# An attention and two-layer mixture-of-experts kernel: VectorE finishes a pair's first block before it converts weights, and the second layer's routing steps move between quarters

## The chip, the core and the metric

The kernel runs on one core of a Trainium2 chip. The metric is device time in microseconds (us) of one execution. Engines are named as in the profile: PE (TensorE), DVE (VectorE), ACT (ScalarE), POOL (GpSimd) and SP (SyncE, which issues the DMAs).

## What is computed

Decayed causal attention over 4608 tokens makes x (4608 x 512). Two mixture-of-experts layers follow. In each a token goes to one of eight experts (the largest of eight logits). Cut to what matters:

```python
def _moe_ref(x, w_gate, w_output_gate, w1, w2):
    logits = x @ w_gate
    e_idx = np.argmax(logits, axis=1)
    ...
    for e in range(E):                       # E = 8, D = 512, F = 1024
        mask = e_idx == e
        h = np.maximum(x[mask] @ w1[e], 0.0)
        ye = h @ w2[e]
        out[mask] = gate_w[mask, None] * eom[mask, e, None] * ye

def reference(**kwargs):
    ...
    x = _moe_ref(x=x, **moe_kwargs)
    return _moe2_ref(x=x, **moe2_kwargs)     # as above, with a bias by modality
```

So the second layer's experts are chosen from the first layer's output, token by token.

## The kernel before

Attention and the first layer's routing take the first 225 us; the change does not touch them. Then `experts` runs sixteen positions `P_`, eight experts of the first layer (`P_ < E`) and eight of the second, with an instruction stream written out per engine; engines meet only in counting semaphores (`take` waits for one and takes it down).

A position's rows are worked in **units**: a pair of 128-row blocks in slot 0, a pair in slot 1, and, where a block is left over, a short unit (slot 2). In these inputs every expert of the first layer has two pairs and a short unit, but expert 5, which has no short unit. A unit goes like this:

- PE computes `ph = w1.x` in four quarters (`quarter(g)`, each 24 matmuls of 256 columns; L991 to L993), then `py = h.w2` for block 0 (`second(0, ...)`, in four parts q of 6 matmuls, part q waiting for quarter q's `h_full`) and for block 1 (`second(1, ...)`; L999 to L1001).
- For each quarter ACT writes the ReLU (L1093) and signals `hh_full`; DVE then evicts the rest into `hT` (L1205) and signals `h_full`. Both engines go through the quarters in order, with other work between.
- `back` ends a block in the first layer: ACT squares `py` (L1081, `ss_full`), DVE makes a scale (`eb`, `v_s`, `f_full`), ACT writes the upper half of the output row (L1084, `x2h_full`), DVE the lower half and signals `x2_rdy`. ACT does not go on to the next block or unit before DVE's `f_full`. In the second layer DVE's part is `final`, three small instructions.
- SP waits for `x2_rdy` and transposes the row back on chip as `x2T`, for the second layer's routing.

**The second layer's routing** of a unit's blocks runs inside the next unit, in four steps: PE's `logits` (L969, needs `x2T`), DVE's `choose` (six small instructions; it gives `l2_full` to ACT and `oh_full` to PE), ACT's `gate` (an exponential), PE's `ranks` (L974, L975, needs `oh_full`) and DVE's `place` (needs `rk_full` from the ranks). `routed` says at which point of a unit each step stands: points 0 to 3 follow quarter g, points 4 to 7 follow part q of `second(0)`. Before the change ACT's and DVE's steps stand at the quarter of the logits.

**Weights** of the next position come in four quarters c of 1 MB into `stg`. ACT makes the upper half (`conv`, L1070), DVE the lower (`conv`, `wb<-stg,wb` of 128 x 2048), which frees that part of `stg` for SP's next load. In slot 0 ACT and DVE convert c = 0 and 1, in slot 1 c = 2 and 3 (`brought`). SP works in program order too: a load that waits for `stg` holds up the transposes behind it.

In slot 0 DVE does both conversions after the fourth eviction and before `back` of block 0:

```python
for q in range(2 - (slot or 0)):
    brought(ve, R_, P_, conv, slot, q + (slot or 0))
if routing or asked(P_, slot):
    ve.sem_inc(T["cnt_ask"])
for b in range(blocks[s]):
    back(s, b) if P_ < E else final(s, b)
```

Of the kernel before, what the change touches and what calls it, by code (L numbers as in the profile page):

```python
# [490 lines left out]
def experts(nc, st, I, K, out):  # L491
# [225 lines left out]
            for q in range(2):  # L717
                brought(eng, R_, P_, conv, 1, q)

    def routed(eng, was, s, sure, at, fn, what=0):  # L720


        plan = {"short": ((1, 3), (3, 7)), "first": ((1, 2), (2, 4), (3, 7)), "pair": (None, (1, 2), (3, 7))}
        for k, p in enumerate(plan["short" if s == 2 else "pair" if sure else "first"]):
            if p and (at is None or p[what] == at):
                if k == 1 or sure:
                    fn(k // 2)
                else:
                    with when(eng, was, "EQ", 2 - k // 2):
                        fn(1)  # L730

    def behind(P_, slot):

# [28 lines left out]
    with nc.Block() as block:  # L762
# [197 lines left out]
        def _(pe):  # L960
            with ExitStack() as rs:
# [20 lines left out]
                def unit(P_, s, w, sure, slot=None, routing=None, counting=False):  # L982
                    two, cs = s < 2, cols(P_, w)
                    if routing is None:
                        routing = behind(P_, slot)

                    def quarter(g):
                        for f in (2 * g, 2 * g + 1):
                            fs, o = slice(f * P, f * P + P), ph[g][:, f % 2, cs]
                            for c in range(4):  # L990
                                pe.matmul(o, w1(P_, 0)[:, c, fs], xT[s][:, c, cs], start=(c == 0), stop=False)  # L991
                                pe.matmul(o, w1(P_, 0)[:, c, fs], xT[s][:, 4 + c, cs], start=False, stop=False)  # L992
                                m = pe.matmul(o, w1(P_, 1)[:, c, fs], xT[s][:, c, cs], start=False, stop=(c == 3))  # L993
                        m.then_inc(T["ph_full"])

                    def second(b, fs):
                        bs = slice(b * P, b * P + P)
                        for f in fs:
                            pe.matmul(py[b], hT[:, 0, f, bs], w2(P_, 0)[:, f, :], start=(f == 0), stop=False)  # L999
                            pe.matmul(py[b], hT[:, 0, f, bs], w2(P_, 1)[:, f, :], start=False, stop=False)  # L1000
                            m = pe.matmul(py[b], hT[:, 1, f, bs], w2(P_, 0)[:, f, :], start=False, stop=(f == 7))  # L1001
                        if f == 7:
                            m.then_inc(T["py_full"])

                    def route(at):
                        if routing:
                            routed(pe, was, s, sure, at, ranks, 1)
                            routed(pe, was, s, sure, at, logits)
                    take(pe, f"x_full{s}", 16)
                    for g in range(4):  # L1010
                        quarter(g)
                        route(g)
                    take(pe, "py_free0")
                    for q in range(4):
                        take(pe, "h_full")
                        if P_ == 0 and q in (0, 2):
                            pe.wait_ge(T[f"w0_full{2 + q // 2}"], 1)
                        second(0, (2 * q, 2 * q + 1))
                        route(4 + q)
                    if P_ < E:  # L1020
                        note(pe, was, s, sure)
                    if two:
                        take(pe, "py_free1")
                        second(1, range(4))
                        if counting:
                            counts(cum)
                        if slot == 0:
                            ahead(pe, R_, P_)
                        second(1, range(4, 8))
                        if asked(P_, slot):  # L1030
                            counts(cums)
# [5 lines left out]
                for P_ in range(NP):  # L1037
                    if P_ == E - 1:
                        take(pe, "ord_pe")
                        learn(pe, R_)  # L1040
                    if P_ == E:
                        take(pe, "w_full", 4)
                        with when(pe, R_["early"], "GT", 0):
                            for k in range(EP):
                                unit(E, k, PAIR, False, routing=k == 0, counting=k == 0)
                        with pe.Else():
                            routed(pe, was, 0, False, None, lambda b: (logits(b), ranks(b)))
                            counts(cum)
                        take(pe, "reg_pe")
                        less_early(pe, R_)  # L1050
                    co.leave(R_, P_)
                    if P_ and P_ != E:
                        take(pe, "w_full", 4)

                    def none(P_=P_):
                        ahead(pe, R_, P_)
                        if P_ == E - 2:
                            counts(cums)
                    walk(co, R_, P_, unit, none)
# [3 lines left out]
        def _(ac):  # L1063
            with ExitStack() as rs:
# [24 lines left out]
                def unit(P_, s, w, sure, slot=None, routing=None):  # L1089
                    cs = cols(P_, w)  # L1090
                    for g in range(4):
                        take(ac, "ph_full")
                        ac.activation(hT[:, 0, 2 * g:2 * g + 2, cs], ph[g][:, :, cs], AF.Relu).then_inc(T["hh_full"])  # L1093
                        if P_ == 0 and slot == 0 and g < 2:
                            conv(0, 2 + g)
                        brought(ac, R_, P_, conv, slot, {(0, 2): 0, (1, 0): 0, (1, 2): 1}.get((slot, g)))
                        if routing or behind(P_, slot):
                            routed(ac, was, s, sure, g, gate)
                    if slot == 0:
                        brought(ac, R_, P_, conv, slot, 1)  # L1100
                    ac.sem_inc(T[f"x_free{s}"])
                    for b in range(blocks[s]):
                        back(P_, s, b)
                    if P_ < E:
                        note(ac, was, s, sure)
# [6 lines left out]
                for P_ in range(NP):  # L1112
                    if P_ == E - 1:
                        take(ac, "ord_ac")
                        learn(ac, R_)
                    if P_ == E:
                        with when(ac, R_["early"], "GT", 0):
                            for k in range(EP):
                                unit(E, k, PAIR, False, routing=k == 0)
                        with ac.Else():  # L1120
                            routed(ac, was, 0, False, None, gate)
                        take(ac, "reg_ac")
                        less_early(ac, R_)
                    co.leave(R_, P_)
                    ahead(ac, R_, P_)
                    walk(co, R_, P_, unit, conv=conv)
# [3 lines left out]
        def _(ve):  # L1130
            ch = Chain(ve, T, "dve")
            tt, ts, stt, tr = ve.tensor_tensor, ve.tensor_scalar, ve.scalar_tensor_tensor, ve.tensor_reduce
            with ExitStack() as rs:
# [64 lines left out]
                def unit(P_, s, w, sure, slot=None, routing=None):  # L1198
                    cs = cols(P_, w)
                    for g in range(4):  # L1200
                        routes = routing or behind(P_, slot)
                        if routes and g < 3:
                            routed(ve, was, s, sure, g, choose)
                        take(ve, "hh_full")
                        stt(hT[:, 1, 2 * g:2 * g + 2, cs], ph[g][:, :, cs], 0.0, hT[:, 0, 2 * g:2 * g + 2, cs], op0=ALU.max, op1=ALU.subtract).then_inc(T["h_full"])  # L1205
                        if routes:
                            if g == 3:
                                routed(ve, was, s, sure, g, choose)
                            routed(ve, was, s, sure, g, place)
                        if P_ == 0 and slot == 0 and g < 2:  # L1210
                            conv(0, 2 + g)
                        if slot == 1 and g == 1:
                            brought(ve, R_, P_, conv, slot, 0)
                    for q in range(2 - (slot or 0)):
                        brought(ve, R_, P_, conv, slot, q + (slot or 0))
                    if routing or asked(P_, slot):
                        ve.sem_inc(T["cnt_ask"])
                    for b in range(blocks[s]):
                        back(s, b) if P_ < E else final(s, b)
                    if asked(P_, slot):  # L1220
                        order()
                    if P_ < E:
# [57 lines left out]
                for P_ in range(NP):  # L1280
# [5 lines left out]
                    if P_ == E:  # L1286
# [2 lines left out]
                            final_counts()  # L1289
                            unit(E, 1, PAIR, False)  # L1290
                        with ve.Else():
                            routed(ve, was, 0, False, None, lambda b: (choose(b), place(b)))
                            ve.sem_inc(T["cnt_ask"])
                            final_counts()
                        less_early(ve, R_)
# [132 lines left out]
```

## Time and profile before

| | |
|---|---|
| median of 3 runs | 1053.33 us (1050.77 to 1054.05) |
| the profiled execution | 1051.67 us, of which the span of instructions is 1049.9 us |
| PE busy | 999.0 us (95%) |
| DVE busy | 465.8 us (44%) |
| ACT busy | 405.0 us (39%) |
| mean granted PE clock | 0.970 of full speed |
| experts, first layer | about 225 to 656 us of the span |
| experts, second layer | from 656 us to the end |

PE is the engine to look at. Where its matmuls follow one another at the rate of their columns (256 columns start 0.109 us apart, 512 columns 0.216 us), a stretch can get no shorter; what can change is the time in which PE waits, and the granted clock.

### The profile page before, as it was taken

How to read it: one execution, taken by the hardware profiler on the slowest of the kernel's cores; microseconds unless marked ns; L12 is line 12 of the kernel's file. 1: busy time of each engine (PE TensorE's matmuls, PEld its weight loads, DVE VectorE, ACT ScalarE, POOL GpSimd, SP SyncE). 2: the span in 40 equal slices, each digit the busy share in tenths (PEclk: the TensorE clock that was granted, in tenths of full speed). 3: DMA queues.
4: the chain of work that ended last, by engine and by line, in shares of the span. 5: the costliest groups of instructions: out<-in, count | busy, mean ns of one | idle time of the engine just before them, and what ended most of it. 6: DMA issues, size and time to landing. Idle time of an engine off the chain costs nothing. (4 is left out here: it accounts for less than half of the span.)

```text
span 1049.9 us, 24162 instructions
## 1 busy us (share of the span) xinstructions
PE 999.0 (95%) x8502; PEld 721.8 (69%) x8502; DVE 465.8 (44%) x1445; ACT 405.0 (39%) x948; POOL 248.0 (24%) x277
## 2 busy tenths in 40 slices
PE   8999998569999999999898999999999999999996
PEld 6998998446766767676665676776677666676673
DVE  3676675746464646565556555414111111112111
ACT  3886785624353525353434253223111121111111
POOL 4455573531121212213122212200110011100110
PEclk9998998779999999999999999999999999999998
DMA  9999999668664566564845465282112113112200
GB/s 298 288 299 288 311 304 287 174 211 234 175 192 99 180 129 176 127 164 134 236 69 155 133 149 161 60 223 61 51 51 50 40 45 59 51 51 51 58 32 23
DMA packets 218130, 154.32 MB, mean 147 GB/s; under 512 B 174569, under 2 KB 174733, under 8 KB 218000
## 3 DMA queue, kind: packets, MB, share of 16 engines
q1 hardware_dynamic: 209040, 124.09, 47.1%
q0 software_dynamic: 8960, 28.62, 7.6%
q8 instruction: 67, 1.10, 0.4%
q14 instruction: 63, 0.52, 0.2%
HBM read 80.21 MB, written 33.92 MB: 109 GB/s over the span
## 5 line engine op out<-in xcount | busy, mean ns | idle before, releaser
L992 PE MATMUL ph<-xT,wb 128*128 128x256 f16 (+2 forms) x1344 | 339.0, 263 | 0.0
L993 PE MATMUL ph<-xT,wb 128*128 128x256 f16 (+2 forms) x1344 | 339.0, 263 | 0.0
L991 PE MATMUL ph<-xT,wb 128*128 128x256 f16 (+2 forms) x1344 | 338.8, 263 | 0.1
L1205 DVE SCALAR_TENSOR_TENSOR hT<-ph,hT 128x512 f16<-128x512 f32 (+2 forms) x168 | 105.4, 637 | 332.1 <-DVEq L464 331.3
L1001 PE MATMUL py<-wb,hT 128*128 128x512 f16 x608 | 230.4, 379 | 0.0
L1000 PE MATMUL py<-wb,hT 128*128 128x512 f16 x608 | 230.4, 379 | 0.0
L999 PE MATMUL py<-wb,hT 128*128 128x512 f16 x608 | 230.3, 379 | 0.0
L1093 ACT ACTIVATE hT<-ph 128x512 f16<-128x512 f32 (+2 forms) x168 | 92.8, 553 | 214.4 <-ACTq L464 214.1
L991 PEld LDWEIGHTS ph<-xT,wb 128*128 128x128 f16 x1344 | 131.8, 98 | 16.6 <-issue 0.5
L992 PEld LDWEIGHTS ph<-xT,wb 128*128 128x128 f16 x1344 | 131.7, 98 | 16.3 <-issue 0.3
L993 PEld LDWEIGHTS ph<-xT,wb 128*128 128x128 f16 x1344 | 131.7, 98 | 12.9
L1331 POOL DMA_INDIRECT out_dram<-yo,idxo x37 | 36.0, 972 | 334.8 <-POOLq L464 319.8
L1001 PEld LDWEIGHTS py<-wb,hT 128*128 128x128 f16 x608 | 59.4, 98 | 71.8
L999 PEld LDWEIGHTS py<-wb,hT 128*128 128x128 f16 x608 | 59.3, 98 | 65.1
L1000 PEld LDWEIGHTS py<-wb,hT 128*128 128x128 f16 x608 | 59.4, 98 | 65.0
L476 DVE SCALAR_TENSOR_TENSOR wb<-stg,wb 128x2048 f16<-128x2048 f32 x38 | 87.0, 2289 | 14.2 <-DVEq L464 14.2
L1320 POOL TENSOR_SCALAR idx<-v_pos 128x1 int32<-128x1 f32 x39 | 16.3, 417 | 314.0 <-POOLq L464 314.0
L1087 ACT ACTIVATE yo<-py,v_gcol 128x512 f32<-128x512 f32 x37 | 25.4, 687 | 168.1 <-ACTq L464 168.1
L306 PE MATMUL po<-vs,a 128*128 128x64 f32 x576 | 76.1, 286 | 2.2 <-POOL a L329 2.2
L306 PEld LDWEIGHTS po<-vs,a 128*128 128x128 f32 x576 | 70.8, 199 | 4.7 <-POOL a L329 2.3
L1070 ACT ACTIVATE wb<-stg 128x2048 f16<-128x2048 f32 x38 | 72.3, 1903 | 1.0 <-ACTq L464 0.9
L337 ACT ACTIVATE xg<-po,cst 128x64 f32<-128x64 f32 x288 | 62.7, 336 | 0.0
(154 smaller groups left out, 967.2 us busy)
## 6 DMA issues: line engine op xcount, KB each, us to landing
stg<-in_moe_w_dram SPq DMA_DIRECT2D x38, 1024.0 KB, 8.5
dkn<-in_dk_dram SPq DMA_DIRECT2D x36, 256.0 KB, 5.3
qn<-in_q_dram SPq DMA_DIRECT2D x36, 256.0 KB, 5.4
vn<-in_v_dram SPq DMA_DIRECT2D x36, 256.0 KB, 5.3
kn<-in_k_dram SPq DMA_DIRECT2D x36, 256.0 KB, 5.6
xs<-zero SPq DMA_DIRECT2D x8, 262.0 KB, 3.0
xs<-zero SPq DMA_DIRECT2D x8, 258.0 KB, 2.4
w0s<-in_moe_w_dram SPq DMA_DIRECT2D x8, 256.0 KB, 3.7
```

The source lines that it names most:

```text
L306: nc.tensor.matmul(o, a, b_, start=m in fresh, stop=ends.get(m) == n)
L337: nc.scalar.activation(self.xg[:, h * HD:(h + 1) * HD], self.po[:, h, :], AF.Identity, scale=col(f"gx{self.c}")[:, h:h + 1])
L476: r = fn(*a, **kw).then_inc(self.sem, 1)
L991: pe.matmul(o, w1(P_, 0)[:, c, fs], xT[s][:, c, cs], start=(c == 0), stop=False)
L992: pe.matmul(o, w1(P_, 0)[:, c, fs], xT[s][:, 4 + c, cs], start=False, stop=False)
L993: m = pe.matmul(o, w1(P_, 1)[:, c, fs], xT[s][:, c, cs], start=False, stop=(c == 3))
L999: pe.matmul(py[b], hT[:, 0, f, bs], w2(P_, 0)[:, f, :], start=(f == 0), stop=False)
L1000: pe.matmul(py[b], hT[:, 0, f, bs], w2(P_, 1)[:, f, :], start=False, stop=False)
L1001: m = pe.matmul(py[b], hT[:, 1, f, bs], w2(P_, 0)[:, f, :], start=False, stop=(f == 7))
L1070: ac.activation(wb[P_ % 2][:, 0, 2048 * c:2048 * c + 2048], stg[:, 2048 * c:2048 * c + 2048], AF.Copy, scale=WS).then_inc(T["cv_full"])
L1093: ac.activation(hT[:, 0, 2 * g:2 * g + 2, cs], ph[g][:, :, cs], AF.Relu).then_inc(T["hh_full"])
L1205: stt(hT[:, 1, 2 * g:2 * g + 2, cs], ph[g][:, :, cs], 0.0, hT[:, 0, 2 * g:2 * g + 2, cs], op0=ALU.max, op1=ALU.subtract).then_inc(T["h_full"])
```

## The change

1. In slot 0 DVE does `back` (or `final`) of block 0 first, then both conversions, then block 1.
2. The points of the routing steps are in a table, apart for each step. A pair in slot 1: block 0's logits go from point 1 to 2, ranks from 2 to 5, choose and gate from 1 to 2, place from 1 to 3; block 1's logits from 3 to 4. Slot 0: the left-over block's logits, choose and gate from 1 to 0, place to 2; block 0's ranks from 4 to 5 and place from 2 to 3; a further block's logits from 3 to 4. A short unit: logits from 3 to 4 (block 0), place of a left-over block from 1 to 3.
3. DVE evicts a quarter before it does `choose` of that point, where it did so after `choose` at the first three.
4. ACT converts c = 1 in slot 0 before the gate of the fourth quarter, not after.

```diff
-        plan = {"short": ((1, 3), (3, 7)), "first": ((1, 2), (2, 4), (3, 7)), "pair": (None, (1, 2), (3, 7))}
-        for k, p in enumerate(plan["short" if s == 2 else "pair" if sure else "first"]):
-            if p and (at is None or p[what] == at):
...
+    WHEN = {
+        "short": ((1, 3, 1, 3), (4, 7, 3, 3)),
+        "first": ((0, 2, 0, 2), (2, 5, 2, 3), (4, 7, 3, 3)),
+        "pair": (None, (2, 5, 2, 3), (4, 7, 3, 3)),
+    }
+    LOGITS, RANKS, CHOOSE, PLACE = range(4)
...
+        for k, p in enumerate(WHEN["short" if s == 2 else "pair" if sure else "first"]):
+            fns = [fn for what, fn in steps if p and at in (None, p[what])]
...
-                        brought(ac, R_, P_, conv, slot, {(0, 2): 0, (1, 0): 0, (1, 2): 1}.get((slot, g)))
+                        brought(ac, R_, P_, conv, slot, {(0, 2): 0, (0, 3): 1, (1, 0): 0, (1, 2): 1}.get((slot, g)))
...
-                    if slot == 0:
-                        brought(ac, R_, P_, conv, slot, 1)
...
-                        if routes and g < 3:
-                            routed(ve, was, s, sure, g, choose)
                         take(ve, "hh_full")
                         stt(hT[:, 1, 2 * g:2 * g + 2, cs], ph[g][:, :, cs], 0.0, hT[:, 0, 2 * g:2 * g + 2, cs], op0=ALU.max, op1=ALU.subtract).then_inc(T["h_full"])
-                        if routes:
-                            if g == 3:
-                                routed(ve, was, s, sure, g, choose)
-                            routed(ve, was, s, sure, g, place)
+                        if routing or behind(P_, slot):
+                            routed(ve, was, s, sure, g, (CHOOSE, choose), (PLACE, place))
...
-                    for q in range(2 - (slot or 0)):
-                        brought(ve, R_, P_, conv, slot, q + (slot or 0))
+                    if slot == 1:
+                        brought(ve, R_, P_, conv, slot, 1)
...
                         back(s, b) if P_ < E else final(s, b)
+                        for q in range(2 if (slot, b) == (0, 0) else 0):
+                            brought(ve, R_, P_, conv, slot, q)
```

DVE at the end of expert 0's slot 0 unit. `hT<-ph3` evicts the fourth quarter, `wb1<-stg` converts, `eb20` to `x2row00` is `back` of block 0, `eb21` begins `back` of block 1. Before:

```order
L1205 SCALAR_TENSOR_TENSOR hT<-ph3,hT 128x512
L476 SCALAR_TENSOR_TENSOR wb1<-stg,wb1 128x2048 x2
L476 TENSOR_SCALAR eb20<-v_ss0 128x1
L476 TENSOR_SCALAR v_s20<-eb20 128x1
L476 TENSOR_TENSOR v_rinv20<-v_s20,meta0 128x1
L476 COPY cur0<-meta0 128x9
L476 RECIPROCAL v_inv20<-v_rinv20 128x1
L476 COPY x2row00<-meta0 128x1
L476 SCALAR_TENSOR_TENSOR x2row00<-py0,v_s20,x2row00 128x512
L476 TENSOR_SCALAR eb21<-v_ss1 128x1
```

And the same place in the change:

```order
L1208 SCALAR_TENSOR_TENSOR hT<-ph3,hT 128x512
L476 TENSOR_SCALAR eb20<-v_ss0 128x1
L476 TENSOR_SCALAR v_s20<-eb20 128x1
L476 TENSOR_TENSOR v_rinv20<-v_s20,meta0 128x1
L476 COPY cur0<-meta0 128x9
L476 RECIPROCAL v_inv20<-v_rinv20 128x1
L476 COPY x2row00<-meta0 128x1
L476 SCALAR_TENSOR_TENSOR x2row00<-py0,v_s20,x2row00 128x512
L476 SCALAR_TENSOR_TENSOR wb1<-stg,wb1 128x2048 x2
L476 TENSOR_SCALAR eb21<-v_ss1 128x1
```

Both conversions stood before block 0's `back` and now stand between the two blocks, so block 1's `back` and the next unit's evictions stand behind them.

DVE in the slot 1 unit of expert 0. `hT<-ph0` to `hT<-ph2` evict quarters, `w_L0` to `oh20` is `choose` of block 0, `v_gq0` begins its `place`. Before:

```order
L1205 SCALAR_TENSOR_TENSOR hT<-ph0,hT 128x512
L476 TENSOR_REDUCE w_L0<-pr0 128x8
L476 SCALAR_TENSOR_TENSOR w_l20<-w_L0,v_inv20,cur0 128x8
L476 TENSOR_REDUCE v_mx0<-w_l20 128x1
L476 SCALAR_TENSOR_TENSOR w_w0<-w_l20,v_mx0,cst 128x8
L476 TENSOR_REDUCE v_m20<-w_w0 128x1
L476 TENSOR_SCALAR oh20<-w_w0,v_m20,cur0 128x8
L1205 SCALAR_TENSOR_TENSOR hT<-ph1,hT 128x512
L476 SCALAR_TENSOR_TENSOR v_gq0<-v_sume0,v_rinv20 128x1
```

And the same place in the change:

```order
L1208 SCALAR_TENSOR_TENSOR hT<-ph0,hT 128x512
L1208 SCALAR_TENSOR_TENSOR hT<-ph1,hT 128x512
L476 SCALAR_TENSOR_TENSOR wb1<-stg,wb1 128x2048
L1208 SCALAR_TENSOR_TENSOR hT<-ph2,hT 128x512
L476 TENSOR_REDUCE w_L0<-pr0 128x8
L476 SCALAR_TENSOR_TENSOR w_l20<-w_L0,v_inv20,cur0 128x8
L476 TENSOR_REDUCE v_mx0<-w_l20 128x1
L476 SCALAR_TENSOR_TENSOR w_w0<-w_l20,v_mx0,cst 128x8
L476 TENSOR_REDUCE v_m20<-w_w0 128x1
L476 TENSOR_SCALAR oh20<-w_w0,v_m20,cur0 128x8
L1208 SCALAR_TENSOR_TENSOR hT<-ph3,hT 128x512
L476 SCALAR_TENSOR_TENSOR v_gq0<-v_sume0,v_rinv20 128x1
```

`choose` of block 0 moved behind the evictions of quarters 1 and 2 and the conversion between them.

## Rows read from the trace of the kernel before

**Rows 1.** Busy time by stretch: PE, PEld, DVE, ACT, POOL, clock, DMA share, GB/s.

```profile
224.73:676.00 451.27, 441.99 (x3673) 304.38 (x3672) 257.44 (x814) 187.91 (x365) 95.19 (x118) 0.99 0.60 158
```

**Rows 2.** Waits of PE by line: total us, times, longest.

```profile
PE pr L969 <- PEq L464: 5.4, 6, 2.6
...
PE pr L974 <- PEq L464: 2.1, 1, 2.1
PE pr L980 <- PEq L464: 1.4, 1, 1.4
```

**Rows 3.** Busy time by stretch, in experts 5 and 6; columns as in rows 1.

```profile
525.05:529.33 4.28, 4.28 (x30) 3.21 (x27) 2.00 (x8) 0.60 (x3) 0.00 (x0) 0.60 0.08 10
...
564.00:566.00 2.00, 0.46 (x4) 0.29 (x4) 1.18 (x3) 0.03 (x1) 1.77 (x1) 1.00 0.00 0
...
577.00:578.00 1.00, 1.00 (x7) 0.69 (x6) 0.52 (x6) 1.00 (x1) 0.34 (x2) 0.50 1.04 414
```

**Rows 4.** Timeline of DVE, end of expert 1's slot 0: start, duration, instruction, [idle].

```profile
296.61 2.29 DVE L476 SCALAR_TENSOR_TENSOR wb<-stg,wb 128x2048 f16<-128x2048 f32 x1 [0.48 <-DVEq L464]
299.38 0.15 DVE L476 TENSOR_SCALAR eb<-v_ss 128x1 int32<-128x1 int32 x1 [0.48 <-DVEq L464]
...
300.80 0.74 DVE L476 SCALAR_TENSOR_TENSOR x2row<-py,v_s,x2row 128x512 f16<-128x512 f32 x1
302.40 0.15 DVE L476 TENSOR_SCALAR eb<-v_ss 128x1 int32<-128x1 int32 x1 [0.85 <-DVEq L464]
```

**Rows 5.** Timeline of ACT, same place and the start of slot 1.

```profile
296.88 0.20 ACT L1081 ACTIVATION_READ_ACCUMULATOR sq<-py 128x1 f32 x1
...
302.92 0.69 ACT L1084 ACTIVATE x2row<-py,v_s 128x512 f16<-128x512 f32 x1 [0.67 <-ACTq L464]
304.18 0.60 ACT L1093 ACTIVATE hT<-ph 128x512 f16<-128x512 f32 x1 [0.58 <-ACTq L464]
304.68 1.90 ACT L1070 ACTIVATE wb<-stg 128x2048 f16<-128x2048 f32 x1
...
307.84 0.20 ACT L1074 ACTIVATE v_nmx<-v_mx 128x1 f32<-128x1 f32 x1 [0.44 <-ACTq L464]
```

**Rows 6.** Timeline of DVE, expert 1's slot 1.

```profile
307.02 0.18 DVE L476 TENSOR_REDUCE w_L<-pr 128x8 f32<-128x24 f32 x1 [1.01 <-DVEq L464]
...
308.27 0.29 DVE L476 TENSOR_SCALAR oh<-w_w,v_m,cur 128x8 f16<-128x8 f32 x1
308.93 0.69 DVE L1205 SCALAR_TENSOR_TENSOR hT<-ph,hT 128x512 f16<-128x512 f32 x1 [0.38 <-DVEq L464]
309.54 0.15 DVE L476 SCALAR_TENSOR_TENSOR v_gq<-v_sume,v_rinv 128x1 f32<-128x1 f32 x1
...
310.42 2.29 DVE L476 SCALAR_TENSOR_TENSOR wb<-stg,wb 128x2048 f16<-128x2048 f32 x1 [0.48 <-DVEq L464]
```

**Rows 7.** Timeline of PE, expert 1's slot 1: the second logits and the second ranks.

```profile
312.01 0.35 PE L969 MATMUL pr<-wg,x2T 128*128 128x24 bf16 x8
...
317.39 0.17 PE L974 MATMUL pr<-oh,tri 128*128 128x8 f16 x1
```

**Rows 8.** Timeline of SP, expert 5: transposes behind the weights' loads.

```profile
516.89 4.06 SPq L819 DMA_TRANSPOSE xT<-xs  x1
521.34 2.61 SPq L805 DMA_TRANSPOSE x2T<-x2row  x2
```

**Rows 9.** Timeline of DVE: the last conversion of expert 5's slot 0; an eviction in expert 6.

```profile
512.49 2.29 DVE L476 SCALAR_TENSOR_TENSOR wb<-stg,wb 128x2048 f16<-128x2048 f32 x1 [0.48 <-DVEq L464]
...
573.90 0.69 DVE L1205 SCALAR_TENSOR_TENSOR hT<-ph,hT 128x512 f16<-128x512 f32 x1 [0.86 <-DVEq L464]
```

**Rows 10.** Timeline of PE: three of its waits (experts 1, 5 and 6).

```profile
328.74 0.35 PE L969 MATMUL pr<-wg,x2T 128*128 128x24 bf16 x8 [0.59 <-PEq L464]
...
524.85 0.35 PE L969 MATMUL pr<-wg,x2T 128*128 128x24 bf16 x8 [2.58 <-PEq L464]
...
576.25 0.17 PE L974 MATMUL pr<-oh,tri 128*128 128x8 f16 x1 [2.14 <-PEq L464]
```

More of the change, by code (lines that the diff above doesn't have):

```diff
@@ L718, in rest, with routed @@
                 brought(eng, R_, P_, conv, 1, q)
-    def routed(eng, was, s, sure, at, fn, what=0):
-        plan = {"short": ((1, 3), (3, 7)), "first": ((1, 2), (2, 4), (3, 7)), "pair": (None, (1, 2), (3, 7))}
-        for k, p in enumerate(plan["short" if s == 2 else "pair" if sure else "first"]):
-            if p and (at is None or p[what] == at):
[L726 to L730, printed above, removed]
+    WHEN = {
[4 more added lines that the diff above has]
+    LOGITS, RANKS, CHOOSE, PLACE = range(4)
+    def routed(eng, was, s, sure, at, *steps):
+        for k, p in enumerate(WHEN["short" if s == 2 else "pair" if sure else "first"]):
+            fns = [fn for what, fn in steps if p and at in (None, p[what])]
+            if not fns:
+                continue
+            each = lambda b: [fn(b) for fn in fns]
+            if k == 1 or sure:
+                each(k // 2)
+            else:
+                with when(eng, was, "EQ", 2 - k // 2):
+                    each(1)
     def behind(P_, slot):
@@ L1006, in route @@
                         if routing:
-                            routed(pe, was, s, sure, at, ranks, 1)
-                            routed(pe, was, s, sure, at, logits)
+                            routed(pe, was, s, sure, at, (RANKS, ranks))
+                            routed(pe, was, s, sure, at, (LOGITS, logits))
                     take(pe, f"x_full{s}", 16)
@@ L1046, in _ @@
                         with pe.Else():
-                            routed(pe, was, 0, False, None, lambda b: (logits(b), ranks(b)))
+                            routed(pe, was, 0, False, None, (LOGITS, logits), (RANKS, ranks))
                             counts(cum)
@@ L1095, in unit @@
                             conv(0, 2 + g)
-                        brought(ac, R_, P_, conv, slot, {(0, 2): 0, (1, 0): 0, (1, 2): 1}.get((slot, g)))
+                        brought(ac, R_, P_, conv, slot, {(0, 2): 0, (0, 3): 1, (1, 0): 0, (1, 2): 1}.get((slot, g)))
                         if routing or behind(P_, slot):
-                            routed(ac, was, s, sure, g, gate)
-                    if slot == 0:
-                        brought(ac, R_, P_, conv, slot, 1)
+                            routed(ac, was, s, sure, g, (CHOOSE, gate))
                     ac.sem_inc(T[f"x_free{s}"])
@@ L1120, in _ @@
                         with ac.Else():
-                            routed(ac, was, 0, False, None, gate)
+                            routed(ac, was, 0, False, None, (CHOOSE, gate))
                         take(ac, "reg_ac")
@@ L1200, in unit @@
                     for g in range(4):
-                        routes = routing or behind(P_, slot)
-                        if routes and g < 3:
-                            routed(ve, was, s, sure, g, choose)
                         take(ve, "hh_full")
                         stt(hT[:, 1, 2 * g:2 * g + 2, cs], ph[g][:, :, cs], 0.0, hT[:, 0, 2 * g:2 * g + 2, cs], op0=ALU.max, op1=ALU.subtract).then_inc(T["h_full"])
-                        if routes:
-                            if g == 3:
-                                routed(ve, was, s, sure, g, choose)
-                            routed(ve, was, s, sure, g, place)
+                        if routing or behind(P_, slot):
+                            routed(ve, was, s, sure, g, (CHOOSE, choose), (PLACE, place))
                         if P_ == 0 and slot == 0 and g < 2:
@@ L1291, in _ @@
                         with ve.Else():
-                            routed(ve, was, 0, False, None, lambda b: (choose(b), place(b)))
+                            routed(ve, was, 0, False, None, (CHOOSE, choose), (PLACE, place))
                             ve.sem_inc(T["cnt_ask"])
```

## The prediction

> **What bounds the kernel now.** I first read busy time by stretch: from 224.73 to 676 us, the first layer's experts, PE is busy 441.99 of 451.27 us at a mean clock of 0.99, DVE 257.44, ACT 187.91 [rows 1]. PE's matmuls follow at the rate of their columns, so only PE's waits and its clock can be won. Then PE's waits by line: three lines belong to the expert part, and all are the second layer's routing: logits 5.4 us in six waits, ranks 2.1 in one, counts (L980) 1.4 in one [rows 2], 8.9 us. PE waits nowhere for an eviction, a ReLU or weights. Third, the clock: behind the 2.58 us wait in expert 5, a quarter of 24 matmuls took 4.28 us at a mean clock of 0.60 [rows 3, 10], where 24 x 0.109 makes 2.62 us. A drop of the clock costs 1.66 us. The 2.14 us wait in expert 6 [rows 10] was followed by another, with 0.50 at 577 us [rows 3]; the wait for counts, in a stretch where PE was busy 0.46 of 2.00 us, was not: the clock is 1.00 there [rows 3].
>
> So the most that the change can win is 8.9 + 2 x 1.66 = 12.2 us, 1.2%. What it can lose depends on how late DVE and ACT, both in program order, come to the steps on which PE waits. I walk one expert (expert 1; the traced times of before are my clock).
>
> **Block 0 ahead of the conversions.** DVE converts from about 293.9 us on, while PE is still at block 0; these conversions fill a time in which DVE has nothing else. ACT's square of block 0 is read out at 296.88 + 0.20 = 297.1 [rows 5]. Now DVE stands idle until then, starts `back` at 297.2, needs 300.80 + 0.74 - 299.38 = 2.16 us for it, then 0.48 to the next instruction [rows 4]: 299.9. A conversion takes 299.38 - 296.61 = 2.77 us with its tail [rows 4], two end at 305.4. Block 1's `back` begins there, not at 302.40 [rows 4]: **3.0 us later**. Block 0's transposed row is there some 2 us sooner; in this expert PE did not wait for it.
>
> ACT is bound to DVE here: its `x2h` of block 1 comes 302.92 - 302.40 = 0.52 after DVE's `eb` [rows 4, 5], so at 305.9, and only 0.69 later, at 306.6, can it start slot 1's first ReLU (304.18 before). Its conversion follows 0.50 later and takes 1.90 [rows 5]: the second ReLU runs from 309.0 to 309.6.
>
> **Later points, evictions first, in slot 1.** DVE evicts quarter 1 at 309.75; 0.61 later (308.93 to 309.54) it converts [rows 6], 2.77 us, evicts quarter 2 at 313.1 and begins `choose` of block 0 at 313.7, where it began at 307.02 [rows 6]. `choose` ends 308.27 + 0.29 - 307.02 = 1.54 after its start [rows 6], 315.25; PE sees it about 0.2 later (an estimate), 315.45. PE wants it at point 5. Its first layer ends at 312.0 as before [rows 7]; part 0 (6 matmuls, 1.29 us), the second logits (0.2) and part 1 bring it to 314.8. **PE waits 0.7 us.**
>
> ACT's gate of block 0 now stands at point 2, ahead of the fourth ReLU. It begins 307.84 - 307.02 = 0.82 after `choose` [rows 5, 6], at 314.5, and holds ACT about 0.7 (estimate from its two instructions): the fourth ReLU ends at 315.8, DVE evicts quarter 3 at 316.0, begins `place` at 316.6 and, 0.88 later (309.54 to 310.42 [rows 6]), `choose` of block 1 at 317.5. That ends at 319.0, PE sees it at 319.2. PE, released at 315.5, has done parts 2 and 3 by 318.1 and wants to rank block 1. **It waits 1.1 us more**; before it ranked at 317.39 without a wait [rows 7].
>
> Sum for a pair in slot 1: 1.8 us. Each is a difference of two chains of some eight hand-offs, whose idle is 0.1 to 0.5 us, so I bound the sum by 0.9 and 2.7. The short unit that follows gives DVE time again: its logits move 1.5 us later on PE, its evictions are not waited for. Experts 0 to 4 and 7 have this shape: 6 x 1.8 = **+10.8 us** (5.4 to 16).
>
> **Expert 5** has no short unit, and there SP's loads and transposes stand in a row: the conversion that ends at 512.49 + 2.29 frees the stage, then comes the load, then `xT` at 516.89 (4.06 us), then `x2T` at 521.34 [rows 8, 9], and PE, waiting since 522.3, gets its logits at 524.85 [rows 10]. The last conversion now ends some 5.7 us later (expert 1: 298.9 to 304.9, and this one started 0.4 late). All of the row moves with it, PE's logits to 530.5. They are wanted one quarter later, at 524.7. PE waits 5.8 instead of 2.6: **+3.2 us** (0 to +5: nothing if the loads, which then meet less traffic, let the transposes start sooner). Here the change makes the row of waits on SP worse which one would think it relieves.
>
> **Expert 6.** `cnt_ask` now comes ahead of the conversions, so PE's 1.4 us for counts goes. DVE comes to slot 1's first eviction at 573.90 as before [rows 9], since there the conversions had already stood close behind block 0; PE, 1.9 us sooner there, waits about 2.8 and 1.1 us for the two ranks in place of 2.1. With the clock's drop mostly inside the second wait I make it **-1.5 us** (-3 to +1).
>
> **What is won.** Besides expert 5's, the longest of the six waits for logits, the six hold 5.4 - 2.6 = 2.8 us [rows 2]. The one in expert 0's slot 1 and those of two short units (0.59 in expert 1 [rows 10]) have 2.0 of it and go, since the rows come sooner or the point is later. The other two, at slot 0's second logits, stay: that point is not moved and the row comes from a short unit, as before. Hand-off gaps of 0.1 at ranks of left-over blocks go too: **-2.3 us** together.
>
> **Costed at nothing:** ACT's order in the fourth quarter of slot 0 (the same unless a gate stands there, which only expert 6 has); the second layer (`final` is three small instructions, conversions there lie under 20 us of matmuls per unit; if they made `final` of block 1 late by 1 us, ACT's output would be late and PE would not wait, having 15 us until it writes that bank again).
>
> **Sum:** 10.8 + 3.2 - 1.5 - 2.3 = +10.2 us. The profiled execution took 1051.67 us, which gives 1061.9; on the median of the three runs, 1.7 above it, 1063.5. I say **1062 us**. A measurement of this kernel tells some 0.3% from no change, 3.2 us.
>
> **The clock.** The rows show drops behind waits of 2.58 and 2.14 us and none behind 1.4. The new waits of 0.7 and 1.1 us have 2.6 us of matmuls between them, so I take none there. The Trainium skill's page "TensorE: Matmul & The Clock Gate" (Part 1) holds that the half clock is the array's resting state, that sustained activity lifts it, and (HAM oscillation) that bursts of matmuls with waits between fall back again and again. By that rule two waits close together could count as one, and the time would be that of the second rival; the trace has no such pair to show it.
>
> **Rivals.**
> 1. **Faster: the waits for routing go and nothing takes their place.** It needs `choose` to be ready 1.8 us sooner than I walked, so that PE's points 5 and 7 have room; the longer room (two parts and a quarter instead of one quarter for block 0) speaks for it, DVE's and ACT's strings against it. If all 8.9 us and both drops go: 1051.7 - 12.2 = 1039.5; with expert 5 left as it is, 1044. It decides at a shift of block 1's `back` of about 1 us, where I find 3.0. Chance 0.10.
> 2. **Slower still: each slot 1 drops the clock.** 6 x 1.66 = 10 us on top, 1072. Against it: the wait of 1.4 us without a drop. Chance 0.15.
> 3. **About the same.** The chains are 1 us shorter than walked: the first wait goes, the second is about 0.7, six of them 4.2; with +3.2 - 1.5 - 2.3 that is +3.6 at most, and +1 if expert 5 pays nothing: 1053 to 1055. Chance 0.13.
>
> My forecast (two short waits in each slot 1) has 0.62, with a range of its own from 1056 to 1067. The range for 8 in 10 takes in rival 3's lower end and rival 2's time: 1052 to 1073. Faster by over 0.3%: 0.10, rival 1. Within: 0.13. Slower: 0.77.
>
> **What the profile of the changed kernel would show.** PE's waits at ranks, one of 2.1 us before, would be some fourteen, of 0.5 to 1.5 us, in pairs, with DVE's `choose` ending just ahead of each. DVE would stand idle some 3 us before `eb` of slot 0's block 0, and its two conversions would lie between the blocks; ACT's first ReLU of slot 1 would come 2 to 3 us later against PE's first quarter. Expert 5's wait for logits would be over 5 us, the wait at counts gone. I am wrong if PE's waits at ranks stay below 4 us in all, or if the second layer's stretch changes by over 1 us.

## The result and the profile after

The changed kernel takes **1062.79 us** (median of 4 runs, 1061.16 to 1066.95) against 1053.37 for the kernel before: a ratio of 1.010 (of the runs' means) with a 95% interval of 1.0066 to 1.0134. It is slower, by 0.7 to 1.3%; the medians lie 9.4 us apart. The forecast was 1062 us, with 0.77 on slower.

Where the time went is best seen by units, from the first matmul of one to the first of the next in PE's timeline (us):

| | before | after |
|---|---|---|
| attention, to the first expert matmul | 224.73 | 224.84 |
| slot 1 of experts 0, 1, 2, 3, 4, 7 | 22.29, 21.34, 21.34, 21.34, 21.34, 21.35 | 22.88, 22.88, 22.87, 23.37, 23.24, 23.20 |
| short units of experts 0 and 1 | 11.70, 11.65 | 10.79, 10.79 |
| short unit of expert 4 | 10.79 | 11.27 |
| expert 5, slot 1 | 25.76 | 29.52 |
| expert 6, slot 0 and slot 1 | 23.20, 25.37 | 21.87, 25.56 |
| all of the first layer's experts | 431.29 | 441.02 |
| the second layer's, to the last matmul | 383.88 | 383.76 |

All of the loss lies in the first layer's experts, +9.73 us. PE's waits after the change, by line as in [rows 2] (L982 is the ranks' line now, L977 the logits'):

```profile
PE pr L982 <- PEq L464: 8.6, 12, 2.5
...
PE pr L977 <- PEq L464: 5.6, 3, 5.1
...
PE pr L982 <- DVEq L483: 1.2, 2, 0.7
...
PE pr L982 <- issue: 0.7, 1, 0.7
```

One wait of 2.1 us at the ranks has become fifteen that hold 10.5 us; the six at the logits have become three, and the longest has grown from 2.6 to 5.1. The wait at counts is gone.

DVE's timeline in expert 1, from the end of slot 0 on, answers to [rows 4, 6]. Slot 1 begins at 300.75 us here, 0.53 earlier than before:

```profile
296.69 0.15 DVE L476 TENSOR_SCALAR eb<-v_ss 128x1 int32<-128x1 int32 x1 [3.17 <-DVEq L464]
...
299.34 2.29 DVE L476 SCALAR_TENSOR_TENSOR wb<-stg,wb 128x2048 f16<-128x2048 f32 x1 [0.48 <-DVEq L464]
302.12 2.29 DVE L476 SCALAR_TENSOR_TENSOR wb<-stg,wb 128x2048 f16<-128x2048 f32 x1 [0.48 <-DVEq L464]
304.89 0.15 DVE L476 TENSOR_SCALAR eb<-v_ss 128x1 int32<-128x1 int32 x1 [0.48 <-DVEq L464]
...
309.62 2.28 DVE L476 SCALAR_TENSOR_TENSOR wb<-stg,wb 128x2048 f16<-128x2048 f32 x1
312.39 0.69 DVE L1208 SCALAR_TENSOR_TENSOR hT<-ph,hT 128x512 f16<-128x512 f32 x1 [0.48 <-DVEq L464]
313.00 0.17 DVE L476 TENSOR_REDUCE w_L<-pr 128x8 f32<-128x24 f32 x1
...
314.24 0.29 DVE L476 TENSOR_SCALAR oh<-w_w,v_m,cur 128x8 f16<-128x8 f32 x1
315.15 0.69 DVE L1208 SCALAR_TENSOR_TENSOR hT<-ph,hT 128x512 f16<-128x512 f32 x1 [0.62 <-DVEq L464]
...
316.55 0.18 DVE L476 TENSOR_REDUCE w_L<-pr 128x8 f32<-128x24 f32 x1 [0.48 <-DVEq L464]
...
317.81 0.29 DVE L476 TENSOR_SCALAR oh<-w_w,v_m,cur 128x8 f16<-128x8 f32 x1
```

DVE stands idle for 3.17 us ahead of block 0's `eb`, the time in which it used to convert, then goes from block to conversions to block to evictions with no gap over 0.74 us. ACT beside it, as in [rows 5]:

```profile
305.41 0.69 ACT L1092 ACTIVATE x2row<-py,v_s 128x512 f16<-128x512 f32 x1 [3.68 <-ACTq L464]
306.00 0.59 ACT L1101 ACTIVATE hT<-ph 128x512 f16<-128x512 f32 x1
306.47 1.91 ACT L1078 ACTIVATE wb<-stg 128x2048 f16<-128x2048 f32 x1
308.27 1.22 ACT L1101 ACTIVATE hT<-ph 128x512 f16<-128x512 f32 x2
...
313.80 0.20 ACT L1082 ACTIVATE v_nmx<-v_mx 128x1 f32<-128x1 f32 x1 [2.51 <-ACTq L464]
...
314.43 0.57 ACT L1101 ACTIVATE hT<-ph 128x512 f16<-128x512 f32 x1
```

ACT waits 3.68 us for DVE's block 1, and later stands 2.51 us at the gate with the fourth ReLU behind it. PE's two ranks come 0.2 us behind the two `oh`, each after a wait (before: none, [rows 7]):

```profile
314.74 0.17 PE L982 MATMUL pr<-oh,tri 128*128 128x8 f16 x1 [0.35 <-PEq L464]
...
318.30 0.17 PE L982 MATMUL pr<-oh,tri 128*128 128x8 f16 x1 [0.66 <-PEq L464]
```

SP in expert 5, as in [rows 8], and PE's wait behind it, as in [rows 10]:

```profile
507.14 20.26 SPq L798 DMA_DIRECT2D stg<-in_moe_w_dram  x4
528.21 3.70 SPq L827 DMA_TRANSPOSE xT<-xs  x1
532.29 2.61 SPq L813 DMA_TRANSPOSE x2T<-x2row  x2
```

```profile
535.91 0.37 PE L977 MATMUL pr<-wg,x2T 128*128 128x24 bf16 x8 [5.11 <-PEq L464]
```

The four loads, which wait for DVE's conversions to free the stage, now spread over 20.26 us (14.93 before); the transposes stand behind them.

### The profile page after: what moved, and what is told of

Its sections match the earlier page's. It is cut to its first block, busy times and chain, and to the rows that moved or that the text cites. A ratio compares the mean times of both kernels' runs of the same rounds, so it can differ in the third digit from the quotient of the medians.

```text
span 1059.4 us, 24154 instructions
## 1 busy us (share of the span) xinstructions
PE 998.4 (94%) x8502; PEld 718.1 (68%) x8502; DVE 465.7 (44%) x1445; ACT 400.6 (38%) x948; POOL 208.5 (20%) x277
## 5 line engine op out<-in xcount | busy, mean ns | idle before, releaser
L1323 POOL TENSOR_SCALAR idx<-v_pos 128x1 int32<-128x1 f32 x39 | 7.6, 194 | 362.5 <-POOLq L464 362.5
```

## The experiments

Theory A: the conversions' move alone makes DVE late, and the later points by themselves give room. Theory B: choosing behind evictions and a conversion is what makes PE wait.

**The points alone.** The changed kernel with the conversions put back:

```diff
-                    if slot == 1:
-                        brought(ve, R_, P_, conv, slot, 1)
+                    for q in range(2 - (slot or 0)):
+                        brought(ve, R_, P_, conv, slot, q + (slot or 0))
...
-                        for q in range(2 if (slot, b) == (0, 0) else 0):
-                            brought(ve, R_, P_, conv, slot, q)
```

> The changed kernel with both conversions of slot 0 put back ahead of block 0's back on DVE; the later points and the evictions ahead of choosing stay. Theory A (the conversions' move makes DVE late, the later points by themselves give room): the pairs of waits at the ranks in slot 1 shrink from about 0.5 and 0.7 us to about 0.2 and 0, the logits of expert 5 wait under 0.5 us (2.6 before, 5.1 in the changed kernel), no clock drop there, the waits of two short units go, expert 6 keeps 3 to 4 us. About 1047 us (1044 to 1051), faster than before. Theory B (choosing behind the evictions and the conversion is what makes PE wait): the pairs of waits stay at 0.4 us or more each, 1058 to 1063 us.

Measured: 1049.66 us (median of 12 runs) against 1053.3, ratio 0.9966 (0.9943 to 0.9989): faster than before, as theory A has it. PE's waits in the first layer's experts:

```profile
PE pr L988 <- PEq L464: 1.7, 1, 1.7
PE pr L977 <- PEq L464: 1.5, 3, 0.7
```

No wait at the ranks is left in this view, which lists idle times over 0.15 us; slot 1 takes 21.62 us in experts 0, 1, 2, 4 and 7 (22.9 to 23.2 in the changed kernel), and expert 5's 22.63. The counts (L988) wait, since `cnt_ask` stands behind the conversions again. Three details came otherwise than expected: expert 5's logits still wait 0.7 us, expert 4's short unit takes 11.60 us (10.79 before), and in expert 6 only the counts wait, 1.7 us, where 3 to 4 us were expected. The run shows the later points and the evictions ahead of choosing together; they were not tested apart.

**The conversions' move alone.** The kernel before with the DVE edit of the change's first point (the diff above the other way round).

> The kernel before with the one edit that DVE does block 0's back ahead of the two conversions in slot 0. Theory A: block 1's back and slot 1's first eviction come 3 us late, choose of block 0 misses point 2, so the first ranks of each slot 1 wait about 1.3 us in six experts (8 us); expert 5's logits, one quarter earlier here than in the changed kernel, wait about 8 us (2.6 before); expert 6's ranks 4 to 5 us (2.1), its counts no longer 1.4. About 1067 us (1062 to 1072). Theory B (the later points are at fault): 1052 to 1056 us, no waits at ranks beyond expert 6's.

Measured: 1072.81 us (4 runs), ratio 1.0176 (1.0137 to 1.0215), 0.8 us above the expected range, on theory A's side. The waits in the first layer's experts:

```profile
PE pr L974 <- PEq L464: 12.8, 7, 4.8
PE pr L969 <- PEq L464: 12.3, 6, 7.6
```

The first ranks of six slots 1 wait 1.2 to 1.5 us each, expert 6's 4.8, expert 5's logits 7.6, all as written. Not foreseen was expert 0's short unit, 15.06 us where it took 11.70 before: its logits wait 2.6 us instead of 0.65, and the clock is at half (0.50) from 278.8 to 282.1 behind them. SP starts `x2T` 2.69 us after the unit's first matmul here, behind an `xT` that ends at 273.09, and 0.98 us after it in the kernel before, where `xT` had ended earlier. With the conversions alone, then before:

```profile
267.55 5.54 SPq L819 DMA_TRANSPOSE xT<-xs  x1
273.59 3.94 SPq L805 DMA_TRANSPOSE x2T<-x2row  x2
```

```profile
260.92 6.47 SPq L819 DMA_TRANSPOSE xT<-xs  x1
269.09 3.83 SPq L805 DMA_TRANSPOSE x2T<-x2row  x2
```

Expert 2's short unit has a new wait of 0.8 us, whose cause stays open; the one of 0.6 in expert 1's was there before. On the old points the conversions' move costs 19.5 us, on the new ones 13.1 (1062.79 against 1049.66): the later points give room, but not enough.

**One conversion on each side of block 0's back:**

```diff
-                    if slot == 1:
-                        brought(ve, R_, P_, conv, slot, 1)
+                    if slot is not None and slot < 2:
+                        brought(ve, R_, P_, conv, slot, slot)
...
-                        for q in range(2 if (slot, b) == (0, 0) else 0):
-                            brought(ve, R_, P_, conv, slot, q)
+                        if (slot, b) == (0, 0):
+                            brought(ve, R_, P_, conv, slot, 1)
```

> The changed kernel with one conversion of slot 0 ahead of block 0's back and one behind it. Theory A: the first conversion lies in DVE's idle time, so block 1's back begins about 0.3 us later than before the change instead of 3, the waits at ranks in slot 1 are about 0.2 us; expert 5's last conversion ends 3 us later than before, its logits wait about 3 us. About 1051 us (1047 to 1055). Theory B: as the changed kernel, 1059 to 1064 us.

Measured: 1051.87 us (10 runs) against 1053.3, ratio 0.9975 (0.9954 to 0.9996).

```profile
PE pr L977 <- PEq L464: 3.4, 3, 2.8
PE pr L982 <- PEq L464: 2.5, 1, 2.5
```

The pairs of waits are gone with only one conversion moved, so it is the second conversion behind the block that makes DVE late. Block 1's `eb` in expert 1 shows the lateness itself. It comes 1.12 us after slot 1's first matmul in the kernel before, 4.14 in the changed kernel and 4.14 with the conversions alone (first row), but 1.65 with the points alone (second) and 1.64 with one conversion on each side (third); slot 1 begins at 307.37, 302.58 and 304.17 in these three:

```profile
311.51 0.15 DVE L476 TENSOR_SCALAR eb<-v_ss 128x1 int32<-128x1 int32 x1 [0.48 <-DVEq L464]
304.23 0.15 DVE L476 TENSOR_SCALAR eb<-v_ss 128x1 int32<-128x1 int32 x1 [0.48 <-DVEq L464]
305.81 0.15 DVE L476 TENSOR_SCALAR eb<-v_ss 128x1 int32<-128x1 int32 x1 [0.48 <-DVEq L464]
```

Expert 5's logits wait 2.8 us, between 0.7 with no conversion moved and 5.1 with both.

**ACT's gate behind the fourth ReLU:**

```diff
-                            routed(ac, was, s, sure, g, (CHOOSE, gate))
+                            routed(ac, was, s, sure, g, (PLACE, gate))
```

> The changed kernel with ACT's gate at the point of place instead of that of choose (in slot 1 behind the fourth ReLU, not ahead of it). It tests the walk's step that the gate holds the fourth ReLU and through it the second choose: if it does, the second wait of each pair at the ranks in slot 1 gets 0.3 to 0.4 us shorter (8 to 9 us of waits at ranks become 6 to 7) while the first stays; slot 0's ranks may wait 0.5 to 0.8 us instead, since place of the left-over block then waits for a later gate. Time 1059 to 1066 us. If the second wait does not move, the gate was no part of its chain.

Measured: 1068.2 us (4 runs), ratio 1.0145 (1.0111 to 1.018), 2 us above the expected range. Expert 1's two ranks in slot 1 and the second ranks in expert 2's slot 0, in PE's timeline:

```profile
316.83 0.17 PE L982 MATMUL pr<-oh,tri 128*128 128x8 f16 x1 [0.34 <-PEq L464]
...
320.15 0.17 PE L982 MATMUL pr<-oh,tri 128*128 128x8 f16 x1 [0.42 <-PEq L464]
...
350.50 0.17 PE L982 MATMUL pr<-oh,tri 128*128 128x8 f16 x1 [0.32 <-PEq L464]
```

The second wait falls from 0.66 to 0.42 and the first stays, so the gate was in the second one's chain, with 0.24 us. Slot 0 pays more than that back: its ranks wait 0.3 to 0.5 us in experts 1 to 5, 0.7 in expert 6 and 1.2 in expert 7, and PE waits 1.7 us at the start of expert 6.

**SP's loads behind the transposes**, for an expert without a short unit. `held` is called behind the next position's first unit, and the usual place of the load keeps it only where there is a short unit:

```diff
+                        def held():
+                            if P_ > 1:
+                                with when(sp, R_["od"][P_ - 1], "EQ", 0):
+                                    next_w(P_ + 1, 0)
...
                         unit(P_, 0, lambda: row(0))
+                        held()
...
                         unit(P_, 2, lambda: row(pairs, P))
+                        if P_ < E - 1:
+                            next_w(P_ + 2, 0)
                         co.to(after)
-                        next_w(P_ + 2, 0)
+                        if P_ == E - 1:
+                            next_w(P_ + 2, 0)
```

On the changed kernel:

> The changed kernel; behind an expert without a short unit SP issues the loads of the next-but-one expert's first two quarters after the next position's transposes and not ahead of them. Theory A (expert 5's 5.1 us wait is the row on SP: conversion, load, xT, x2T): the wait at the logits of expert 5 goes to under 0.5 us and with it the clock drop behind it; expert 5's slot 1 takes about 23 us instead of 29.5, the pairs of waits at the ranks stay as they are. About 1056 us (1053 to 1059). Rival (the block's row itself is late, or the transposes wait for the DMA rings): the wait stays over 3 us, 1060 us or more.

Measured: 1058.94 us (10 runs) against 1052.35, ratio 1.0079 (1.0045 to 1.0113), at the edge of the expected range. SP in expert 5, and what PE waits for in all:

```profile
516.35 2.74 SPq L827 DMA_TRANSPOSE xT<-xs  x1
523.91 9.43 SPq L813 DMA_TRANSPOSE x2T<-x2row  x2
```

```profile
PE pr L994 <- PEq L464: 8.7, 12, 2.5
PE ph L1011 <- PEq L464: 1.6, 1, 1.6
```

No wait at the logits is left, and the ranks (L994) wait as in the changed kernel, 8.7 us for 8.6. So the row on SP was expert 5's wait. Its slot 1 takes 24.59 us, not 23, since 1.6 us of a new wait stand at expert 6's first matmul.

**The same on the points alone:**

> The later points with the conversions where they were before, and SP's loads behind the transposes as in the run with the changed kernel. Theory A: only what was left of expert 5's wait goes (0.7 us, slot 1 from 22.6 to about 21.7 us), all else as in the points-only run: 1047 to 1050 us, faster than before and than the change by over 10 us. Rival (loads that come later hold up the next conversion): a wait for the weights at expert 7 or late evictions in expert 6, 1051 us or more.

Measured: 1047.75 us (12 runs) against 1052.35, ratio 0.9968 (0.9937 to 0.9999). Expert 5's wait is gone, but the one of 1.6 us at expert 6's start is there as well, so that expert 5's slot 1 takes 23.35 us, not 21.7. Two ranks wait 0.8 and 0.7 us in expert 6's slot 1, where the points-only run had none (why, see the last section). Like the points-only kernel (ratio 0.9966) it beats the changed kernel by far and the kernel before by little; the two can't be told apart.

## Why the prediction was right, step by step

- **DVE's lateness.** Block 1's `eb` was walked to 305.4 on the clock of before; slot 1 starts 0.53 earlier, so 304.87, and the trace has 304.89. ACT's second ReLU was walked to 308.5 and came at about 308.3, `choose` of block 0 to 313.2 (313.00), of block 1 to 317.0 (316.55).
- **The pair of waits.** Sized at 0.7 and 1.1 us. The gaps between the matmuls on either side, beyond their columns, are 0.5 to 0.9 for the first and 0.7 to 0.8 for the second: the second was too large by 0.3. The units give the whole: slot 1 grew by 1.54, 1.53, 2.03, 1.90 and 1.85 us in experts 1, 2, 3, 4 and 7 and by 0.59 in expert 0, where a gap of 0.95 went: 10.4 us with it, forecast 10.8. The points alone show no such wait and the conversions alone do, so the step that decides, "3.0 us later", is shown by the runs: `eb` is 3.02 us later in both kernels with the move, and 0.5 without it.
- **Expert 5.** Forecast +3.2, measured 29.52 - 25.76 = +3.8. The wait grew by 2.5 us, less than the 3.2 walked. The rest is mostly a term that the sum put at nothing: the clock's drop behind the wait is longer, 6.75 us at half clock where it was 3.37 before (first two rows below). With the loads behind the transposes the wait is gone, which shows the row on SP.
- **Expert 6.** Forecast -1.5, measured 47.43 - 48.57 = -1.1. The ranks wait 2.5 and 0.7 us. I took it that the clock drops again; it did not (third row).
- **What is won.** 0.91 and 0.86 us in the short units of experts 0 and 1 and 0.95 in expert 0's slot 1 make 2.7 us. The slot 0 units apart from expert 6's give 1.0 more, of it 0.56 in expert 7, whose wait for logits was forecast to stay. That is 3.8 us, forecast 2.3. 0.5 is given back in expert 4's short unit, whose logits now wait; that was not foreseen.
- **The second layer** was costed at nothing and moved by 0.12 us.
- **The sum.** The terms make 10.4 + 3.8 - 1.1 - 3.8 + 0.5, with their decimals the measured +9.73 us, against +10.2. Each was off by 0.4 to 1.5 us, and the errors cancel in part: that the total agrees to 0.5 us is partly luck. The mechanism and the order of the terms are not. (In rival 3, 4.2 - 1.5 - 2.3 is +0.4, not +1; nothing hangs on it.)

Busy time by stretch, columns as in rows 1: the changed kernel in expert 5, the kernel before in expert 5, the changed kernel in expert 6:

```profile
534.70:541.45 6.75, 5.54 (x33) 3.98 (x34) 1.65 (x7) 0.60 (x3) 0.00 (x0) 0.50 0.25 45
525.62:528.99 3.37, 3.37 (x18) 2.39 (x16) 1.77 (x7) 0.60 (x3) 0.00 (x0) 0.50 0.02 2
590.00:594.00 4.00, 2.90 (x14) 1.23 (x14) 2.56 (x13) 1.44 (x7) 0.69 (x3) 1.00 0.91 249
```

Of the rivals, the second (a drop in each slot 1) fell: in the six slots 1 that it spoke of, no pair of waits dropped the clock, in the changed kernel or in the run with the later gate. The first, faster, would have needed what the points-only run has: block 1's `back` about where it was (1.65 us after slot 1's first matmul, 1.12 before). The third needed chains 1 us shorter than walked; they were 0.2 to 0.4 us shorter, and the first wait of each pair was there.

## What to carry to other kernels

Work that an engine does while it would wait anyway is free; moved behind the thing waited for, it costs its full time to all that stands behind it, here 5.5 us of conversions against 2.5 us that are free (block 0 is done by 299.9, block 1's `back` began at 302.40), 3 us late. Fill the idle time first and move only what does not fit: one conversion on each side lost nothing in the pairs, though expert 5, where SP's row hangs on the last conversion, took 24.56 us against 22.63. Walk an in-order engine's string by the clock of one unit, with the tails between dependent instructions, before a step is moved "ahead"; here that gave block 1's start to 0.02 us and each wait of a pair to 0.4 us.

## What the runs showed of the hardware that I had not expected

Whether the clock drops behind a wait of some 2 us does not hang on its length alone. In expert 6 a wait of 2.1 us was followed by half clock in the kernel before; one of 2.5 was not in the changed kernel, but was in the run with one conversion on each side and in the one with the loads behind on the changed kernel. The points-only run dropped at the wait of 1.7 us for counts, the same with the loads behind did not. Busy time by stretch behind these waits: one conversion on each side, the loads behind on the changed kernel, the points alone, and the points with the loads behind:

```profile
584.60:587.95 3.35, 3.35 (x9) 1.13 (x8) 1.68 (x12) 0.60 (x3) 1.39 (x3) 0.50 0.44 100
589.45:592.80 3.35, 3.35 (x9) 1.17 (x8) 1.91 (x12) 0.59 (x3) 1.39 (x3) 0.50 0.52 117
566.00:569.30 3.30, 3.30 (x17) 2.38 (x16) 1.93 (x10) 1.92 (x4) 0.00 (x0) 0.50 0.28 89
565.00:569.30 4.30, 4.30 (x41) 3.86 (x40) 2.75 (x12) 2.92 (x6) 0.00 (x0) 1.00 0.46 114
```

Nor does a drop always cost its time. Expert 6's slot 1 takes 23.30 us in both of the last two: with the drop PE waits nowhere over 0.15 us at the ranks, without it 0.8 and 0.7 us. With the drop behind the 2.5 us wait it takes 26.17 us in the run with the loads behind and 25.56 without the drop in the changed kernel, 0.6 apart and not 1.7, since the second wait at the ranks is gone. One execution of each kernel was traced, so how often a drop comes is not shown.

Three runs (the later gate, and both with the loads behind) have 1.6 to 1.7 us of wait at expert 6's first matmul, behind the jump over a short unit that is not there; the last conversion that it waits for had ended 1.6 us before PE came to it in the last of them (534.99 + 2.29 = 537.28 against 538.92), and the transpose of its rows had been issued over 25 us before in the first two (531.25 against 556.63, 516.35 against 550.25). What it is stays open.
